# Threshold attention and a two-layer projection: TensorE in 64-row tiles from the fourth quad on, projections in two phases of half rows

## The chip, the cores and the metric

One core of one Trainium2 chip. The metric is the device time of one execution in microseconds (us), median of the runs. A run more than 1.5% above the fastest of its kernel counts as slow and is left out of ratios, though not out of the medians. The experiments ran in three sets, on three chips, so between sets only the ratios compare, each to the kernel before in the same rounds.

## The reference

Attention over 8 batches of 8 heads, 576 positions, head size 64. Scores further than tau = 0.02 below their row's maximum are set to -1e9 ahead of the softmax. The result, 4608 tokens of 512, goes through two projections with a gate between.

```python
scores = scale * q @ k.T
thresh = max(scores, -1) - tau
scores = where(scores >= thresh, scores, -1e9)
attn = exp(scores - max(scores)); attn /= attn.sum(-1) + 1e-9
x = (attn @ v)                      # to tokens x 512
h = x @ w_in                        # 512 -> 2048
g = h * clip(h + 3, 0, 6) / 6
out = g @ w_out                     # 2048 -> 512
```

## The kernel before

Two heads make a pair, two pairs a quad; there are 16 quads. A quad has nine slots, each with the scores of 128 query rows for two heads (the ninth has the last 64 rows of all four heads, and no first-projection item). All engines work through the slots in order, and each slot carries pieces of other work: one item of the first projection (two 128-row blocks of h, 256 or 320 tokens wide), a quarter of an output tile of the second projection, a key transpose or an attention product.

```python
# scores: contraction over 64, two heads at once in two 64-row tiles of the array
nc.tensor.matmul(tiles[a][:, hf, 0:HALF], qT_of(pair)[a*64:(a+1)*64, t*P:(t+1)*P], keys(pair, a, hf), ...)

def mm1(item, pool=None):                       # first projection, full 128 rows
    hps = (pool or ps_h).tile([P, 2, 512], F32, ...)      # the one h buffer, two banks
    for n in range(2):
        for ki in range(KI):
            nc.tensor.matmul(hps[:, n, 0:w], w_in_sb[:, ki, ...], xT[b][:, ki, c0:c0 + w], ...)

# slot n, in the order of the text (each engine keeps its own part of it)
sm_exp(prev); sm_max(sl)                        # ACT; DVE maxima, GpSimd bias
h = mm1(item); r = mm1_relu(h, on_act=...); mm1_gate(item, h, r)   # PE; ACT or DVE; DVE
sm_recip(prev)                                  # DVE
mm2_part(bb, mt, part)                          # PE, a quarter of an output tile
sm_mask(sl)                                     # ACT, waits for the bias
# ... key transpose or attention product, and its eviction
queue[n + 1].tiles = scores(...)                # PE
sm_norm(prev)                                   # GpSimd
```

The program lays out PSUM, the memory that TensorE writes its results to, in this way: four banks for scores, two for h, one for output tiles, one for transposes and attention products.

## Time and profile before

| | before |
|---|---|
| time, median of 3 runs | 562.7 us (562.25 to 563.66) |
| span of the profiled run | 562.3 us |
| busy share PE / ACT / DVE / GpSimd | 95% / 84% / 75% / 54% |
| a quad in the middle of the run | 31.4 us, of which PE 31, ACT 28.4 to 29.1 |

How to read it: the records of TensorE's products overlap (in the prediction's lines, a group that starts at 301.62 and lasts 1.25 us is still on when the next starts at 302.71), so 95% says that TensorE seldom stands still, not that it multiplies at its peak. PE is TensorE, ACT ScalarE, DVE VectorE and POOL GpSimd; `h<-xT,w_in_sb` reads "writes h from xT and w_in_sb". The lines themselves are in the prediction.

### The profile page before, as it was taken

The page shows a single profiled execution, that of the slowest core. Times are in us where ns is not written, and L with a number is a line of the kernel's source. Part 1 is how long each engine was busy: PE and PEld are TensorE (multiplying, and loading weights), DVE is VectorE, ACT ScalarE, POOL GpSimd, SP SyncE. Part 2 cuts the span into 40 slices and gives each one's busy share as a digit, 9 for nine tenths or more (in the row PEclk, how much of TensorE's full clock was granted, in tenths as well). Part 3 has the DMA queues.
Part 4 walks back from the last instruction along what each step waited for, and adds up shares of the span by engine and source line. Part 5 has one row for each costly group of instructions (what it writes and reads, how often), then busy time and mean ns, then how long its engine had stood idle before and what let it go on. Part 6 is the DMA issues. An engine that isn't in the chain of part 4 may idle for free.

```text
span 562.3 us, 11634 instructions
## 1 busy us (share of the span) xinstructions
PE 535.0 (95%) x3856; PEld 309.3 (55%) x3856; DVE 424.4 (75%) x1040; ACT 470.3 (84%) x999; POOL 305.2 (54%) x646
## 2 busy tenths in 40 slices
PE   7998798899999999999999999999999999999997
PEld 5665455455545565555555565655555565654663
DVE  3588787687878788787878798887978798883440
ACT  4799899798988999989898999899898999983540
POOL 1678878854556555655456555755556555561000
PEclk8899999899999999999999999999999999999999
DMA  5879999997689876978589867987699865453102
GB/s 110 135 110 166 162 160 184 207 148 144 112 159 153 151 153 127 208 139 155 114 150 170 159 137 146 174 160 146 127 137 175 167 124 117 101 109 86 38 20 75
DMA packets 286204, 77.52 MB, mean 138 GB/s; under 512 B 269248, under 2 KB 281536, under 8 KB 286144
## 3 DMA queue, kind: packets, MB, share of 16 engines
q1 hardware_dynamic: 268736, 67.86, 64.8%
q0 software_dynamic: 17408, 8.92, 13.7%
q8 instruction: 30, 0.49, 0.4%
q14 instruction: 30, 0.25, 0.2%
HBM read 36.70 MB, written 9.44 MB: 82 GB/s over the span
## 4 chain that ended last, share of the span: by engine, by line
PE 58%; DVE 11%; ACT 9%; issue 4%; POOL 1%; DMA 1%; SPq 1%; DVEq 0%; POOLq 0%
PE h L353 18%; PE o L382 17%; PE s L256 16%; DVE s L277 5%; ACT s L285 4%; PE av L323 3%; ACT s L290 3%; DVE g L370 2%; DVE r L364 2%; ACT r L362 2%; PE s L262 1%; PE tp L213 1%; PE ar L323 1%; DVE osb L390 1%; POOL pn L298 1%
## 5 line engine op out<-in xcount | busy, mean ns | idle before, releaser
L298 POOL TENSOR_SCALAR pn<-s,rinv 128x576 bf16<-128x576 f32 x288 | 211.6, 745 | 133.5 <-issue 58.5
L277 DVE TENSOR_SCALAR_CACHE_REDUCE s<-s 128x576 f32<-128x576 f32 x288 | 205.9, 752 | 44.9 <-PE s L256 35.2
L285 ACT ACTIVATE s<-s,bias 128x576 f32<-128x576 f32 x288 | 207.1, 766 | 36.8 <-POOL bias L280 35.7
L290 ACT ACTIVATE s<-s 128x576 f32<-128x576 f32 x288 | 192.7, 671 | 0.3
L256 PE MATMUL s<-kT,qT 64*128 64x288 f32 x1024 | 172.7, 435 | 5.4 <-DVE s L277 3.2
L353 PE MATMUL h<-xT,w_in_sb 128*128 128x320 bf16 (+1 forms) x1024 | 145.0, 287 | 5.5 <-DVE g L370 4.6
L382 PE MATMUL o<-w_out_sb,g 128*128 128x512 bf16 x576 | 140.9, 379 | 3.6 <-DVE osb L390 3.0
L353 PEld LDWEIGHTS <-w_in_sb 128*128 128x128 bf16 x1024 | 92.0, 97 | 68.4 <-issue 31.1
L256 PEld LDWEIGHTS s<-kT,qT 64*128 64x128 f32 x1024 | 94.8, 188 | 62.7 <-DVE s L277 24.9
L370 DVE SCALAR_TENSOR_TENSOR g<-r,h 128x512 bf16<-128x512 f32 (+1 forms) x128 | 96.4, 754 | 41.2 <-ACT r L362 39.3
L280 POOL TENSOR_SCALAR bias<-m 128x1 f32<-128x1 f32 x288 | 54.4, 189 | 69.0 <-DVE s L277 48.2
L382 PEld LDWEIGHTS <-g 128*128 128x128 bf16 x576 | 55.6, 98 | 58.2 <-issue 9.8
L362 ACT ACTIVATE r<-h,three 128x640 f32<-128x640 f32 (+1 forms) x74 | 54.4, 737 | 21.1 <-PE h L353 20.4
L290 ACT ACTIVATION_READ_ACCUMULATOR s<-s 128x1 f32 x288 | 54.2, 188 | 0.0
L364 DVE TENSOR_SCALAR r<-h 128x512 f32<-128x512 f32 (+1 forms) x54 | 40.5, 751 | 0.0
L390 DVE TENSOR_SCALAR osb<-o 128x512 f32<-128x512 f32 x31 | 21.0, 676 | 22.2 <-PE o L382 22.2
L323 PE MATMUL av<-pT,vm 128*64 128x512 bf16 x256 | 34.6, 392 | 2.0 <-ACT kT L203 2.0
L323 PEld LDWEIGHTS <-vm 128*64 128x64 bf16 x512 | 18.1, 111 | 25.2 <-issue 18.3
L293 DVE RECIPROCAL rinv<-rsum 128x2 f32<-128x2 f32 x144 | 23.0, 160 | 10.2 <-ACT s L290 9.5
L335 DVE CAST xT<-av 128x512 bf16<-128x512 f32 x32 | 21.8, 681 | 5.6 <-PE av L326 5.3
L277 DVE DVE_READ_ACCUMULATOR s<-s 128x1 f32 x288 | 23.9, 83 | 0.0
L388 ACT ACTIVATE osb<-o 128x512 f32<-128x512 f32 x5 | 3.0, 597 | 23.9 <-PE o L382 23.9
(42 smaller groups left out, 255.9 us busy)
## 6 DMA issues: line engine op xcount, KB each, us to landing
km<-in_k_dram SPq DMA_DIRECT2D x64, 128.0 KB, 3.0
out_dram<-osb SPq DMA_DIRECT2D x32, 256.0 KB, 2.4
nq<-in_q_dram SPq DMA_DIRECT2D x96, 72.0 KB, 2.7
vm<-in_v_dram POOLq DMA_DIRECT2D x16, 256.0 KB, 5.4
nq<-in_q_dram SPq DMA_DIRECT2D x16, 128.0 KB, 3.9
w_in_sb<-in_moe_w_in_dram POOLq DMA_DIRECT2D x16, 128.0 KB, 4.1
w_out_sb<-in_moe_w_out_dram POOLq DMA_DIRECT2D x16, 128.0 KB, 4.5
pT<-pn SPq DMA_TRANSPOSE x119, 3.4
```

Of the source, the lines that this page charges most:

```text
L256: nc.tensor.matmul(tiles[a][:, hf, 0:HALF], qT_of(pair)[a * 64:(a + 1) * 64, t * P:(t + 1) * P], keys(pair, a, hf), start=True, stop=True)
L277: nc.vector.tensor_scalar(out=sl.s[:, i, :].rearrange("p (a b) -> p a b", a=2), in0=ps[:, :, 0:HALF], scalar1=1.0, scalar2=None, op0=Alu.m ...
L280: nc.gpsimd.tensor_scalar(out=sl.bias[:, i:i + 1], in0=sl.m[:, i:i + 1], scalar1=-scale, scalar2=tau, op0=Alu.mult, op1=Alu.add)
L285: nc.scalar.activation(out=s, in_=s, func=Act.Prelu, bias=sl.bias[:, i:i + 1], scale=scale, alpha=REJECT)
L290: nc.scalar.activation(out=s, in_=s, func=Act.Exp, accum_out=sl.rsum[:, i:i + 1])
L298: nc.gpsimd.tensor_scalar(out=pn[:, i, :], in0=sl.s[:, i, :], scalar1=sl.rinv[:, i:i + 1], scalar2=1.0, op0=Alu.mult, op1=Alu.mult)
L323: nc.tensor.matmul(ps[a * 64:(a + 1) * 64, :], vm[:, 2 * hp + a, c * D:(c + 1) * D], pT[:, 5 * a + c, cols], start=(c == 0), stop=False)
L353: nc.tensor.matmul(hps[:, n, 0:w], w_in_sb[:, ki, (ni + n) * P:(ni + n + 1) * P], xT[b][:, ki, c0:c0 + w], start=(ki == 0), stop=(ki == KI ...
L362: nc.scalar.activation(out=r, in_=hps, func=Act.Relu, bias=three[:])
L364: nc.vector.tensor_scalar(out=r, in0=hps, scalar1=3.0, scalar2=0.0, op0=Alu.add, op1=Alu.max)
L370: nc.vector.scalar_tensor_tensor(out=gbuf[:, ni:ni + 2, c0:c0 + w], in0=r, scalar=6.0, in1=hps, op0=Alu.min, op1=Alu.mult)
L382: nc.tensor.matmul(o_ps[0], gbuf[:, ni, mt * P:(mt + 1) * P], w_out_sb[:, ni, :], start=(ni == 0), stop=(ni == NI - 1))
```

## The change

The scores use 64-row tiles of the array and all else uses full rows, so TensorE changes its mode twice in every slot. The intent is to keep it in 64-row tiles. Every projection is cut into half rows: row tile 0 and row tile 1 work at the same time into two different banks, then, in a second phase, they swap banks. Between the phases a product must wait for the end of the other tile's products. That wait goes by way of GpSimd: an empty instruction there waits for TensorE, and TensorE waits for it. To fill the wait, other products stand between the two phases.

```diff
+    class Banks:
+        def products(self, phase, insts):
+            follows(insts[0], self)
+            if self.phase not in (None, phase):
+                relay = nc.gpsimd.nop(nofuse=True)
+                tc.add_manual_dep(relay.ins, self.after.ins.name, SYNC, reason="end of a phase")
+                tc.add_manual_dep(insts[0].ins, relay.ins.name, SYNC, reason="next phase")
+            self.phase, self.after = phase, None
+    def mm1_phase(item, hps, phase):
+        for ki in range(KI):
+            for a in range(2):
+                n, c = a ^ phase, row_tile(a)
+                # hps[:, n] += w_in_sb[c, ki, block ni + n].T @ xT[c, ki, tokens]
+        h_banks.products(phase, insts)
+    # mm2_phase: the same for an output tile, in two halves of 256 columns
 # ... slot n, late slots (n >= 27):
+            elif slot == 5:
+                small.append(lambda: av_main(2 * quad - 1))
+                small.append(lambda: av_rest(quad - 1))
+        if late_slot and slot in (0, 3) and todo2:      # first half of an output tile
+        elif late_slot and slot in (1, 4) and mine:     # its second half
+        elif late_slot and slot == 6 and item and len(todo2) > 1:   # a whole one
+        if late_slot and (phases or small):
+            mm1_phase(item, h, 0)
+            mm2_phase(*phases[0][0], phases[0][1], nis)     # or
+            for job in small: evicts.append(job())          # transposes, attention products
+            mm1_phase(item, h, 1)
+            mm2_phase(*phases[-1][0], phases[-1][1], ...)
+        elif item:
+            h = mm1(item)
-            sm_recip(prev)         # behind the gate
+            sm_recip(prev)         # ahead of relu and gate
 # ... relus on ACT in slots 0, 1, 3, 5 become 0, 1, 4, 5; banks "o" and "m" become one tile of two banks
```

More of the change, by code (lines that the diff above doesn't have):

```diff
@@ L43 @@
     N1 = 22
-    N2 = 28
+    N2 = 27
+    DH = d_model // 2
     scale = 1.0 / math.sqrt(D)
@@ L63 @@
     ps_o = ctx.enter_context(tc.psum_pool(name="ps_o", bufs=1))
-    ps_m = ctx.enter_context(tc.psum_pool(name="ps_m", bufs=1))
     ctx.enter_context(tc.manual_schedule())
@@ L189, with bank, row_tile, __init__ @@
     turn = 0
-    def bank(name):
+    obank = ps_o.tile([P, 2, 512], F32, tag="o", name="o")
+    def bank():
         nonlocal turn
         turn += 1
-        if now < N2 and turn % 2:
-            return ps_o.tile([P, 512], F32, tag="o", name=name)
-        return ps_m.tile([P, 512], F32, tag="m", name=name)
+        return obank[:, turn % 2, :]
+    def row_tile(a):
+        return slice(64 * a, 64 * a + 64)
+    SYNC = mybir.DependencyInfo(mybir.DependencyClass.Sync, mybir.DependencyReason.DATA)
+    groups = []
+    class Banks:
+        def __init__(self):
+            self.phase = self.after = None
+            groups.append(self)
+        def products(self, phase, insts):
[5 more added lines that the diff above has]
+            self.phase, self.after = phase, None
+    def follows(inst, banks=None):
+        for one in groups:
+            if one is not banks and one.after is None:
+                one.after = inst
+    h_banks, o_banks = Banks(), Banks()
     def copy_out(out, in_):
@@ L209, in main_pe @@
     def main_pe(src, pair):
-        ps = bank("tp")
+        ps = bank()
         n = pair % 2
@@ L219, in transpose_q @@
             ps = main_pe(nq[:, 0:1024].rearrange("p (t h d) -> p t h d", h=4, t=4), pair)
-            return lambda: nc.vector.tensor_copy(out=qT_of(pair)[:, 0:512], in_=ps[:])
+            return lambda: nc.vector.tensor_copy(out=qT_of(pair)[:, 0:512], in_=ps)
         n = pair % 2
@@ L224, in transpose_k @@
     def transpose_k(pair):
-        ps = main_pe(nat[pair // 2][1], pair)
-        return lambda: copy_out(kT_of(pair)[:, 64:576], ps[:])
+        if now < N2:
+            ps = main_pe(nat[pair // 2][1], pair)
+            return lambda: copy_out(kT_of(pair)[:, 64:576], ps)
+        km, n = nat[pair // 2][1], pair % 2
+        insts = []
+        for t in range(4):
+            for a in range(2):
+                c = row_tile(a)
+                insts.append(nc.tensor.transpose(obank[:, a, t * 64:(t + 1) * 64],
+                                                 km[c, t, 2 * n:2 * n + 2, :], identf[c, c]))
+        o_banks.products(0, insts)
+        return lambda: copy_out(kT_of(pair)[:, 64:576].rearrange("p (t a j) -> p a t j", a=2, j=64),
+                                obank[:, :, 0:256].rearrange("p a (t j) -> p a t j", j=64))
     def transpose_rest(quad):
-        ps = bank("tr")
         nq, _, kr = nat[quad]
-        nc.tensor.transpose(ps[:, 0:P], kr[:], identf[:])
-        if by_pe(2 * quad):
-            nc.tensor.transpose(ps[:, P:2 * P], nq[:, 1024:1152], identf[:])
+        qT, kT = qkT[quad]
+        if now < N2:
+            ps = bank()
+            nc.tensor.transpose(ps[:, 0:P], kr[:], identf[:])
+            if by_pe(2 * quad):
+                nc.tensor.transpose(ps[:, P:2 * P], nq[:, 1024:1152], identf[:])
+            both = ps.rearrange("p (w n t) -> p w n t", n=2, t=64)
+            rest = both[:, 0]
+        else:
+            o_banks.products(0, [nc.tensor.transpose(obank[:, a, 256:320], kr[row_tile(a), :],
+                                                     identf[row_tile(a), row_tile(a)]) for a in range(2)])
+            rest = obank[:, :, 256:320]
         def evict():
-            qT, kT = qkT[quad]
-            both = ps[:].rearrange("p (w n t) -> p w n t", n=2, t=64)
             if by_pe(2 * quad):
                 nc.vector.tensor_copy(out=qT[:, :, 512:S], in_=both[:, 1])
-            copy_out(kT[0:64, :, S:S + 64], both[0:64, 0])
-            copy_out(kT[64:P, :, 0:64], both[64:P, 0])
+            copy_out(kT[0:64, :, S:S + 64], rest[0:64])
+            copy_out(kT[64:P, :, 0:64], rest[64:P])
         return evict
@@ L255, in scores @@
                 for a in range(2):
-                    nc.tensor.matmul(tiles[a][:, hf, 0:HALF], qT_of(pair)[a * 64:(a + 1) * 64, t * P:(t + 1) * P],
-                                     keys(pair, a, hf), start=True, stop=True)
+                    inst = nc.tensor.matmul(tiles[a][:, hf, 0:HALF], qT_of(pair)[a * 64:(a + 1) * 64, t * P:(t + 1) * P],
+                                            keys(pair, a, hf), start=True, stop=True)
+                    follows(inst)
             else:
@@ L261, in scores @@
                         pair = 2 * quad + n
-                        nc.tensor.matmul(tiles[a][n * 64:(n + 1) * 64, hf, 0:HALF],
-                                         qT_of(pair)[a * 64:(a + 1) * 64, 512:S], keys(pair, a, hf),
-                                         start=True, stop=True)
+                        inst = nc.tensor.matmul(tiles[a][n * 64:(n + 1) * 64, hf, 0:HALF],
+                                                qT_of(pair)[a * 64:(a + 1) * 64, 512:S], keys(pair, a, hf),
+                                                start=True, stop=True)
+                        follows(inst)
         return tiles
@@ L322, in av @@
             for a in range(2):
-                nc.tensor.matmul(ps[a * 64:(a + 1) * 64, :], vm[:, 2 * hp + a, c * D:(c + 1) * D],
-                                 pT[:, 5 * a + c, cols], start=(c == 0), stop=False)
+                inst = nc.tensor.matmul(ps[a * 64:(a + 1) * 64, :], vm[:, 2 * hp + a, c * D:(c + 1) * D],
+                                        pT[:, 5 * a + c, cols], start=(c == 0), stop=False)
+                follows(inst)
         for a in range(2):
@@ L331, in av_main @@
             xT[b] = x_pool.tile([P, KI, S], BF16, tag="xT", name="xT")
-        ps = bank("av")
-        av(ps[:], pair, pts[pair], slice(0, 512))
+        ps = bank()
+        av(ps, pair, pts[pair], slice(0, 512))
         o0 = 64 if b % 2 else 0
-        nc.vector.tensor_copy(out=xT[b][:, hp, o0:o0 + 512], in_=ps[:])
+        return lambda: nc.vector.tensor_copy(out=xT[b][:, hp, o0:o0 + 512], in_=ps)
     def av_rest(quad):
         b, g = divmod(quad, 2)
-        ps = bank("ar")
+        ps = bank()
         for n in range(2):
@@ L342, in av_rest @@
         o0 = 0 if b % 2 else 512
-        nc.vector.tensor_copy(out=xT[b][:, 2 * g:2 * g + 2, o0:o0 + 64],
-                              in_=ps[:, 0:P].rearrange("p (a b) -> p a b", a=2))
+        return lambda: nc.vector.tensor_copy(out=xT[b][:, 2 * g:2 * g + 2, o0:o0 + 64],
+                                             in_=ps[:, 0:P].rearrange("p (a b) -> p a b", a=2))
     def mm1(item, pool=None):
@@ L355, in mm1 @@
         return hps[:, :, 0:w]
+    def mm1_phase(item, hps, phase):
+        b, ni, c0, w = item
+        insts = []
+        for ki in range(KI):
+            for a in range(2):
+                n, c = a ^ phase, row_tile(a)
+                insts.append(nc.tensor.matmul(
+                    hps[:, n, 0:w], w_in_sb[c, ki, (ni + n) * P:(ni + n + 1) * P], xT[b][c, ki, c0:c0 + w],
+                    start=(phase == 0 and ki == 0), stop=(phase == 1 and ki == KI - 1)))
+        h_banks.products(phase, insts)
     def mm1_relu(hps, on_act):
@@ L371, in mm1_gate, with mm2_phase, mm2_full, mm2_out @@
                                        op0=Alu.min, op1=Alu.mult)
-    o_ps = {}
-    def mm2_part(bb, mt, part, pool=None):
-        if part == 0:
-            if pool:
-                o_ps[0] = pool.tile([P, 2, 512], F32, tag="s", name="o")[:, 0, :]
-            else:
-                o_ps[0] = ps_o.tile([P, d_model], F32, tag="o", name="o")[:]
-        for ni in range(part * 4, part * 4 + 4):
-            nc.tensor.matmul(o_ps[0], gbuf[:, ni, mt * P:(mt + 1) * P], w_out_sb[:, ni, :],
+    def mm2_phase(bb, mt, phase, nis):
+        insts = []
+        for ni in nis:
+            for a in range(2):
+                j, c = a ^ phase, row_tile(a)
+                insts.append(nc.tensor.matmul(
+                    obank[:, j, 0:DH], gbuf[c, ni, mt * P:(mt + 1) * P], w_out_sb[c, ni, j * DH:(j + 1) * DH],
+                    start=(phase == 0 and ni == 0), stop=(phase == 1 and ni == NI - 1)))
+        o_banks.products(phase, insts)
+    def mm2_full(bb, mt, ps):
+        for ni in range(NI):
+            nc.tensor.matmul(ps, gbuf[:, ni, mt * P:(mt + 1) * P], w_out_sb[:, ni, :],
                              start=(ni == 0), stop=(ni == NI - 1))
-    def mm2_out(bb, mt, on_act):
+    def mm2_out(bb, mt, on_act, ps=None):
         osb = o_pool.tile([P, d_model], F32, tag="osb", name="osb")
+        dst = osb[:]
+        if ps is None:
+            ps, dst = obank[:, :, 0:DH], dst.rearrange("p (j c) -> p j c", j=2)
+            o_banks.phase = None
         if on_act:
-            nc.scalar.activation(out=osb[:], in_=o_ps[0], func=Act.Copy, scale=1.0 / 6.0)
+            nc.scalar.activation(out=dst, in_=ps, func=Act.Copy, scale=1.0 / 6.0)
         else:
-            nc.vector.tensor_scalar_mul(out=osb[:], in0=o_ps[0], scalar1=1.0 / 6.0)
+            nc.vector.tensor_scalar_mul(out=dst, in0=ps, scalar1=1.0 / 6.0)
         b0 = 2 * bb * S
@@ L412, in moe_of @@
                 items.append(((b, ni, c0, w), ()))
-            items[-1] = (items[-1][0], [(b // 2, mt, part) for mt in mts for part in range(4)])
+            items[-1] = (items[-1][0], [(b // 2, mt) for mt in mts])
         return items
@@ L431 @@
     queue[0].tiles = scores(0, 0)
-    prev = None
+    prev = mine = None
     for n, sl in enumerate(queue):
@@ L447 @@
             load_v(b + 1)
+        copies = pe_transpose(queue[n - 2]) if n > 1 and queue[n - 2].on_chip else None
+        late_slot = n >= N2
+        nxt = 2 * quad + 2
+        more = quad + 1 < NQUAD
+        vector, small = [], []
+        if slot == (6 if late_slot else 5) and more:
+            alloc_qk(quad + 1)
+            vector.append(lambda: transpose_q(nxt))
+        if late_slot:
+            if slot == 0:
+                vector.append(lambda: transpose_q(2 * quad + 1))
+            elif slot == 2:
+                small.append(lambda: transpose_k(2 * quad + 1))
+            elif slot == 5:
+                small.append(lambda: av_main(2 * quad - 1))
+                small.append(lambda: av_rest(quad - 1))
+            elif slot == 7 and more:
+                small.append(lambda: transpose_k(nxt))
+                small.append(lambda: transpose_rest(quad + 1))
+        else:
+            if slot == (1 if quad else 2):
+                vector.append(lambda: transpose_q(2 * quad + 1))
+            elif slot == (2 if quad else 3):
+                small.append(lambda: transpose_k(2 * quad + 1))
+            elif slot == 3 and quad > 0:
+                small.append(lambda: av_main(2 * quad - 1))
+            elif slot == 4 and quad > 0:
+                small.append(lambda: av_rest(quad - 1))
+            elif slot == 6:
+                small.append(lambda: transpose_k(nxt))
+            elif slot == 7:
+                small.append(lambda: transpose_rest(quad + 1))
@@ new lines @@
+        if slot == 8:
+            small.append(lambda: av_main(2 * quad))
+        item = None
+        if slot != 8 and todo1:
+            item, then = todo1.pop(0)
+        phases = []
+        if late_slot and slot in (0, 3) and todo2:
+            mine = todo2.pop(0)
+            phases = [(mine, 0)]
+        elif late_slot and slot in (1, 4) and mine:
+            phases, mine = [(mine, 1)], None
+        elif late_slot and slot == 6 and item and len(todo2) > 1:
+            one = todo2.pop(0)
+            phases = [(one, 0), (one, 1)]
@@ new lines @@
+        evicts = []
+        if late_slot and (phases or small):
+            if item:
+                h = ps_h.tile([P, 2, 512], F32, tag="h", name="h")
+                mm1_phase(item, h, 0)
+            if phases:
+                nis = range(16 if len(phases) == 2 else 4)
+                mm2_phase(*phases[0][0], phases[0][1], nis)
+            for job in small:
+                evicts.append(job())
+            if item:
+                mm1_phase(item, h, 1)
+                h = h[:, :, 0:item[3]]
+            if phases:
+                mm2_phase(*phases[-1][0], phases[-1][1], range(nis.stop % NI, NI))
+        elif item:
+            h = mm1(item)
@@ L451 @@
         sm_max(sl)
-        if slot != 8 and todo1:
-            item, then = todo1.pop(0)
-            h = mm1(item)
-            r = mm1_relu(h, on_act=(slot in (0, 1, 3, 5)))
-            mm1_gate(item, h, r)
-            todo2.extend(then)
-        copies = pe_transpose(queue[n - 2]) if n > 1 and queue[n - 2].on_chip else None
         if prev is not None:
@@ L463 @@
             copies()
+        if item:
+            r = mm1_relu(h, on_act=(slot in ((0, 1, 4, 5) if late_slot else (0, 1, 3, 5))))
+            mm1_gate(item, h, r)
+            todo2.extend(then)
         outs = []
-        pieces = 0 if slot == 3 else 1
-        if slot == 0:
-            second = True
-        if second and slot < 2 and len(todo2) > 1 and todo2[0][1] == todo2[1][1]:
-            pieces, second = 2, False
-        for _ in range(pieces):
-            if todo2:
-                bb, mt, part = todo2.pop(0)
-                mm2_part(bb, mt, part)
-                if part == 3:
-                    outs += mm2_out(bb, mt, on_act=False)
+        for one, phase in phases:
+            if phase == 1:
+                outs += mm2_out(*one, on_act=False)
         for i in range(2):
             sm_mask(sl, i)
-        evict = None
-        nxt = 2 * quad + 2
-        if slot == (1 if quad else 2):
-            evict = transpose_q(2 * quad + 1)
-        elif slot == (2 if quad else 3):
-            evict = transpose_k(2 * quad + 1)
-        elif slot == 3 and quad > 0:
-            av_main(2 * quad - 1)
-        elif slot == 4 and quad > 0:
-            av_rest(quad - 1)
-            if quad % 2 == 0:
-                todo1.extend(moe_of(quad // 2 - 1))
-        elif slot in (5, 6, 7) and quad + 1 < NQUAD:
-            if slot == 5:
-                alloc_qk(quad + 1)
-                evict = transpose_q(nxt)
-            elif slot == 6:
-                evict = transpose_k(nxt)
-            else:
-                evict = transpose_rest(quad + 1)
-        elif slot == 8:
-            av_main(2 * quad)
-        if evict:
+        for job in vector:
+            evict = job()
+            if evict:
+                evict()
+        if not late_slot:
+            evicts = [job() for job in small]
+        for evict in evicts:
             evict()
+        if slot == (5 if late_slot else 4) and quad > 0 and quad % 2 == 0:
+            todo1.extend(moe_of(quad // 2 - 1))
         if n + 1 < len(queue):
@@ L535, in rest2 @@
         while todo2:
-            bb, mt, part = todo2.pop(0)
-            mm2_part(bb, mt, part, pool=ps_s if count[1] % 3 else None)
-            if part == 3:
-                flush()
-                late.extend(mm2_out(bb, mt, on_act=(count[1] % 2 == 0)))
-                count[1] += 1
+            one = todo2.pop(0)
+            c = count[1] % 4
+            ps = ps_s.tile([P, 2, 512], F32, tag="s", name="o")[:, 0, :] if c % 2 else obank[:, c // 2, :]
+            mm2_full(*one, ps)
+            flush()
+            late.extend(mm2_out(*one, on_act=(count[1] % 2 == 0), ps=ps))
+            count[1] += 1
     for item in todo1:
         rest1(*item)
-    av_main(2 * last + 1)
+    av_main(2 * last + 1)()
     rest2()
-    av_rest(last)
+    av_rest(last)()
     for item in moe_of(B - 1):
```

## The prediction

> **What bounds the kernel now.** I read the page first (busy shares, the 40 slices, the chain that ended last), then the stretches of five quads in the middle of the run, then the chain and the timeline of a few slots. A quad is 4 heads of one batch; it has 9 slots, each a tile of softmax scores for two heads, with a first-projection item and a piece of the second projection hung into it.
>
> ```profile
> PE 535.0 (95%) x3856; PEld 309.3 (55%) x3856; DVE 424.4 (75%) x1040; ACT 470.3 (84%) x999; POOL 305.2 (54%) x646
> ```
>
> TensorE is busy nearly all the time, but ScalarE is not far behind. The stretches run from one quad's last score tile to the next one's:
>
> ```profile
> 282.44:313.76 31.32, 31.20 (x230) 17.70 (x229) 26.17 (x65) 28.41 (x63) 19.10 (x39) 1.00 0.99 157
> 376.18:408.10 31.92, 31.89 (x230) 17.55 (x229) 26.76 (x64) 29.14 (x63) 16.68 (x37) 1.00 0.70 142
> ```
>
> The columns after the length are busy us of PE, weight loads, DVE, ACT and POOL. A quad takes about 31.4 us (mean of the last twelve), PE is busy for all of it, ACT for 28.4 to 29.1. ACT's records overlap a little; by start-to-start times a slot costs ACT 2.66 (two exps 1.33, two masks 1.33), and with four relus (0.63) and the key copies (1.45 a quad) 28.0 a quad. That is the floor however fast TensorE gets: 3.4 us a quad could be gained at most.
>
> The chain of waits agrees that TensorE's own order sets the pace:
>
> ```profile
> 317.71 1.17 PE s L256 x8
> 318.88 0.98 PE h L353 x8
> 319.86 1.73 PE o L382 x8
> 321.59 1.17 PE s L256 x8
> 322.76 0.98 PE h L353 x8
> 323.74 0.86 PE o L382 x4
> ```
>
> Scores (s), first projection (h), second projection (o), nothing between. Beside it runs a loop through the only h buffer: projection, relu, gate, next projection. Its terms:
>
> ```profile
> 299.94 0.77 ACT L362 ACTIVATE r<-h,three 128x640 f32<-128x640 f32 x1
> 300.75 0.82 DVE L370 SCALAR_TENSOR_TENSOR g<-r,h 128x640 bf16<-128x640 f32 x1 [1.11 <-ACT r L362]
> 301.62 1.25 PE L353 MATMUL h<-xT,w_in_sb 128*128 128x320 bf16 x8
> 302.71 0.38 PE L382 MATMUL o<-w_out_sb,g 128*128 128x512 bf16 x1
> ```
>
> Relu start to gate start 0.81, gate start to the next projection 0.87, a 320-wide projection 1.09 in TensorE time, its last result some 0.17 after that: 2.9 us (3.0 where DVE does the relu). TensorE's own slot is longer, 1.17+1.09+0.86 = 3.1 and more, so the loop is hidden today.
>
> **What the Trainium skill says.** "TensorEngine Tiling (Array Packing)", Key Properties: changing the tiling mode drains TensorE. The trace agrees: score pairs (64-row tiles) start 0.242 us apart, but from the last pair to the first full-row projection it is 0.335, so 0.09 goes to the drain. On the way in, the last 512-column product holds 0.216 and the first pair starts 0.309 later (0.09 again), and the second pair comes 0.347 after the first, as its weights could not be loaded ahead (0.105 more). A round trip costs 0.29 us. The same page, Gotcha 1: different row tiles cannot write one PSUM bank at the same time. Hence the two phases with a wait between; no run yet shows it. "TensorE: Matmul & The Clock Gate", What overlaps and what doesn't: matmuls end in order, which lets the wait be hung on the first matmul after a phase. "Advanced Engine Details and Errata", Sequencer Loop: control instructions run in the sequencer while engine instructions sit in the queue; so GpSimd's relay should not have to wait for its 0.745 us normalisations to end. The trace before has no relay.
>
> **The change part by part.** The first three quads hardly change (they have no second projection), nor does the tail: one first-projection item more is left for it (+1.1), a quarter of a 3.45 us output tile less (-0.9). So the case is decided by 13 quads.
>
> Removed: mode switches. In the built program 80 of the 106 projection items of the loop run in half rows. Seven slots a quad lose up to 0.29 us, those with attention products (128x64 mode, slots 5 and 8) keep theirs, and slots 3 and 4 fall back to full rows in 10 of 13 quads, as no output tile is waiting. That leaves 4 to 5 slots, 1.3 us a quad. Key transposes in half rows: 0.44 becomes some 0.22 twice, 0.4 a quad. On TensorE alone -1.7 us a quad, -22 us in all.
>
> Unchanged on TensorE: the products. A pair of half-row matmuls should hold the array as long as one full-row matmul (score pairs start 7 ns apart): an output tile is 32 pairs x 0.109 = 3.49 against 16 x 0.216 = 3.45.
>
> Added: 187 relays. Each asks for the first result of the following group (0.27 after its start) plus two semaphore hops, which I put at 0.2. Behind it lie 0.44 us of other products in slots 0 and 1, 0.22 in slot 2. So 0.1 to 0.3 us of stall five times a quad: about +1.
>
> Moved: this is what decides. The products between the two phases now stretch the h loop, and the output tiles are bunched: slots 0 and 1 take one, slot 6 a whole one in every quad. I take for each slot the longer of TensorE's own work and the h loop, 320-wide items, two output tiles a quad:
> slots 0 and 1: 1.09 + half a tile 1.74 + scores 0.97 + relay 0.1 = 3.9 each (loop 3.46);
> slot 2: loop 1.09+0.22+0.3+0.17+0.85+0.86 = 3.4;
> slots 3 and 4: loop 3.0 each;
> slot 5: both attention products lie between the phases (1.10+0.36, switches 0.2), so the loop is 1.09+1.66+0.17+0.80+0.86 = 4.6, and ACT, which does this relu, waits for it;
> slot 6: 1.09+3.49+0.97 = 5.55, plus 0.3 as its output banks must first be emptied by DVE (0.59+0.20 after the gate, against half an item 0.54), 5.9;
> slots 7 and 8: 1.09+0.28+0.3+0.97 and 1.10+0.28+0.97 = 5.0, plus about 0.7 because slot 8's attention product goes to the banks that ACT empties only after slot 7's masks.
> Sum 7.8+3.4+6.0+4.6+5.9+5.7 = 33.4. Quads with 256-wide items are shorter (8 x 0.22 on projections), those with a third tile longer in slots 3 and 4 (2 x 0.8). Weighing them, about 32.7 against 31.4 now. The same rule gives 31.5 for today's kernel. So 13 x 1.3 = +17 us: 580.
>
> **The rivals.** First, TensorE's own work is the pace: then 13 x (-1.7 + 1.0 of relay stalls), -9 us, or with relays fully hidden -22: 541 to 554. For it speak the 95% busy share and the chain; against it that ACT is within 3 us of the bound and that with one h buffer TensorE can't run ahead of gates. Slot 6 has 5.9 us of TensorE work against 2.7 of ACT's, slots 7 and 8 4.7 against 6.3, and neither can store that up. Second, GpSimd's relays become the wait: they stand ahead of the bias in its order, and ACT's masks wait for the bias already.
>
> ```profile
> ACT s L285 <- POOL bias L280: 35.7, 72, 1.9
> ```
>
> If a relay takes 0.5 instead of 0.2, five a quad, that is 13 x 1.5 = +20 more, near 600. Against that: the reciprocal moves ahead of the gate on DVE, so normalisations start earlier and leave the way to the bias free, which could give some of the 35.7 back. Third, half-row weight loads (97 ns each, two per 109 ns) might not overlap; an output tile would then take nearly twice its time, +3.5 a quad per tile and more: over 650. The score loads start 6 ns apart in the trace, so I give this 3%.
>
> **Range and chances.** The slot sums say 580. A careful rearrangement of this size was hardly made without a reason to expect a gain, and the sums take waits one at a time, so I shade to 577. One us per quad is 13 us: the low end, 547, is the first rival at -1.2 a quad, the high end, 599, is the sum with slower relays. The 2% marks are 551.4 and 574.0. Faster 0.2, same 0.25, slower 0.55.
>
> **What would show it.** Right: quads near 32.7 us; slot 6 near 6 us and slots 3 and 4 near 3; new TensorE idle time before h (waiting for gates), before the attention product of slot 8 (waiting for key copies) and before second halves (waiting for GpSimd); ACT's share down, with relus waiting for h in slot 5; score pairs still 0.242 apart but no 0.29 lost in slots 0, 1, 2 and 7; half-row pairs 0.109 apart. Wrong: quads under 30.6 with TensorE busy throughout (first rival), relays stalling TensorE 0.5 us or more (second), pairs spaced 0.2 apart (third).

## The result, and the profile after

The changed kernel takes 591.4 us (median of 4 runs, 585.2 to 597.3) against 562.7: it is slower. The ratio is 1.047, with a 95% interval of 1.039 to 1.055. Ratios here are the mean time of one kernel's fast runs over that of the other's of the same rounds, so not quite the ratio of the medians. One of the four runs (597.3) is slow and not in it. The profiled run is a fast one. First the busy shares of its page:

```profile
PE 533.5 (90%) x5949; PEld 377.0 (64%) x5952; DVE 427.6 (73%) x1041; ACT 468.8 (79%) x998; POOL 305.2 (52%) x646
```

TensorE's busy sum is practically what it was, in 27 us more time. Two quads from the middle, in the same columns as before (length, then busy us of PE, weight loads, DVE, ACT, POOL):

```profile
395.23:429.28 34.05, 30.86 (x383) 22.22 (x378) 26.95 (x65) 28.94 (x63) 16.63 (x37) 1.00 0.71 130
429.28:462.96 33.68, 30.65 (x384) 22.04 (x378) 26.69 (x65) 28.95 (x63) 19.35 (x41) 1.00 0.86 149
```

A quad takes 34 us, ACT is busy for the same 29, and PE is no longer busy for all of it. By the start times of the score products the 27.5 us between the two profiles divide so: up to the fourth quad +1.5, the fourth quad itself +4.2 (35.5 to 39.7), the eleven quads after it +19.2, the last one +1.8, the tail +0.7. The first of these cannot be put down to the change: among the profiles of kernels that share the changed kernel's way up to there it took from 91.0 to 94.0 us, and before 92.5.

The mean length of a slot over those eleven quads, from the last score product of one slot to that of the next:

| slot | 0 | 1 | 2 | 3 | 4 | 5 | 6 | 7 | 8 | sum |
|---|---|---|---|---|---|---|---|---|---|---|
| before | 3.84 | 3.29 | 3.56 | 3.58 | 3.64 | 3.15 | 3.66 | 3.27 | 3.58 | 31.55 |
| after | 3.71 | 3.71 | 2.86 | 3.23 | 3.19 | 3.81 | 6.54 | 3.03 | 3.23 | 33.30 |

Slots 5 and 6 lose 0.66 and 2.88 us and slot 1 loses 0.42, more than the others win. A slot does not hold the same work before and after: slot 1 now has half an output tile and mostly had a quarter, slot 6 has a whole one, slot 5 has both attention products, which were in slots 3 and 4. So the table shows where the quad grew, and not yet why. The time in which TensorE stood idle ahead of its products is plainer: 0.5 us a quad before and 2.4 after. Of these, 0.3 each in slots 3 and 4, 0.2 in slot 5 and 0.75 in slot 6 are nearly all waits for a gate, and 0.8 in slot 8 is the attention product waiting for ACT's key copies.

First a slot that went as intended, slot 0 of a quad, on TensorE's timeline (start, length, instruction):

```profile
332.74 0.60 PE L417 MATMUL h<-xT,w_in_sb 64*128 64x256 bf16 x8
333.18 0.60 PE L443 MATMUL o<-w_out_sb,g 64*128 64x256 bf16 x8
333.61 0.60 PE L417 MATMUL h<-xT,w_in_sb 64*128 64x256 bf16 x8
334.05 1.48 PE L443 MATMUL o<-w_out_sb,g 64*128 64x256 bf16 x24
335.36 1.14 PE L307 MATMUL s<-kT,qT 64*128 64x288 f32 x8
336.33 0.60 PE L417 MATMUL h<-xT,w_in_sb 64*128 64x256 bf16 x8
```

Four pairs of half-row products take 0.44 us, 0.109 a pair, so the two row tiles do work side by side. The second phase (333.61) comes when the 0.43 us of other work is done, so the relay is hidden. From scores to projection it is 0.97 where it was 1.17: the mode switch is gone. Now slots 5 and 6 of the same quad, again TensorE alone:

```profile
350.37 0.62 PE L417 MATMUL h<-xT,w_in_sb 64*128 64x256 bf16 x8
350.92 1.05 PE L376 MATMUL o<-pT,vm 128*64 128x512 bf16 x8
351.81 0.38 PE L380 MATMUL o<-pT,vr 128*64 128x512 bf16 x2
...
352.43 0.61 PE L417 MATMUL h<-xT,w_in_sb 64*128 64x256 bf16 x8
352.88 1.14 PE L307 MATMUL s<-kT,qT 64*128 64x288 f32 x8
354.55 0.89 PE L417 MATMUL h<-xT,w_in_sb 64*128 64x256 bf16 x8 [0.53 <-DVE g L435]
355.35 1.92 PE L443 MATMUL o<-w_out_sb,g 64*128 64x256 bf16 x32
357.09 0.62 PE L417 MATMUL h<-xT,w_in_sb 64*128 64x256 bf16 x8
357.53 1.93 PE L443 MATMUL o<-w_out_sb,g 64*128 64x256 bf16 x32
359.27 1.15 PE L307 MATMUL s<-kT,qT 64*128 64x288 f32 x8
```

Slot 5's item begins at 350.37 and its second phase only at 352.43, as both attention products lie between. What hangs on it is on ACT's and DVE's timelines:

```profile
353.09 0.69 ACT L427 ACTIVATE r<-h,three 128x512 f32<-128x512 f32 x1 [1.44 <-PE h L417]
353.81 0.69 DVE L435 SCALAR_TENSOR_TENSOR g<-r,h 128x512 bf16<-128x512 f32 x1 [1.63 <-ACT r L427]
354.41 0.68 DVE L389 CAST xT<-o 128x512 bf16<-128x512 f32 x1
355.01 0.28 DVE L397 CAST xT<-o 128x128 bf16<-128x128 f32 x1
355.21 0.75 DVE L330 TENSOR_SCALAR_CACHE_REDUCE s<-s 128x576 f32<-128x576 f32 x1
```

ACT stands idle 1.44 us for h, DVE 1.63 for the relu. Then TensorE waits 0.53 us for the gate, which frees h. The evictions of the attention products (the two CASTs) are behind the gate in DVE's order, and the maxima of slot 6, whose scores had ended at 354.02, before the gate did, are behind those. The chain of waits shows the same place in the quad before, one link after another (start, length, link):

```profile
318.38 0.67 PE h L417 x8
...
319.07 0.80 ACT r L427
...
320.64 0.68 DVE xT L389
321.32 0.21 DVE xT L397
321.53 0.04 issue
321.57 1.92 PE o L443 x32
```

Before, such a stretch of the chain was TensorE alone. Here ACT and DVE stand in it.

### The profile page after: what moved, and what is told of

It reads as the page before. It is cut to its first block, busy times and chain, and to the rows that moved or that the text cites. A ratio compares the mean times of both kernels' runs of the same rounds, so it can differ in the third digit from the quotient of the medians.

```text
span 589.8 us, 15943 instructions
## 1 busy us (share of the span) xinstructions
PE 533.5 (90%) x5949; PEld 377.0 (64%) x5952; DVE 427.6 (73%) x1041; ACT 468.8 (79%) x998; POOL 305.2 (52%) x646
## 4 chain that ended last, share of the span: by engine, by line
PE 50%; DVE 14%; ACT 13%; issue 5%; DMA 2%; POOL 1%; SPq 0%; DVEq 0%; POOLq 0%
PE o L443 16%; PE h L417 9%; PE s L307 9%; DVE s L330 6%; ACT s L338 6%; PE h L407 5%; PE o L376 5%; PE o L450 5%; DVE g L435 3%; ACT r L427 3%; ACT s L343 3%; DVE r L429 2%; ACT kT L237 2%; DMA pR<-pn 2%; DVE xT L389 1%
## 5 line engine op out<-in xcount | busy, mean ns | idle before, releaser
L307 PEld LDWEIGHTS s<-kT,qT 64*128 64x128 f32 x1024 | 104.8, 189 | 41.1 <-DVE s L330 17.6
L417 PE MATMUL h<-xT,w_in_sb 64*128 64x256 bf16 (+1 forms) x1280 | 107.2, 284 | 15.7 <-DVE g L435 10.6
L443 PE MATMUL o<-w_out_sb,g 64*128 64x256 bf16 x1792 | 112.6, 269 | 0.9 <-DVE xT L397 0.6
L443 PEld LDWEIGHTS <-g 64*128 64x128 bf16 x1792 | 94.3, 94 | 7.9 <-issue 2.3
L417 PEld LDWEIGHTS <-w_in_sb 64*128 64x128 bf16 x1280 | 61.9, 94 | 45.5 <-issue 21.7
L407 PE MATMUL h<-xT,w_in_sb 128*128 128x320 bf16 (+1 forms) x384 | 53.0, 288 | 12.1 <-DVE g L435 12.0
L407 PEld LDWEIGHTS <-w_in_sb 128*128 128x128 bf16 x384 | 35.4, 98 | 33.1 <-DVE g L435 17.2
L376 PE MATMUL o<-pT,vm 128*64 128x512 bf16 x256 | 34.6, 391 | 11.2 <-ACT kT L237 10.8
L376 PEld LDWEIGHTS <-vm 128*64 128x64 bf16 x512 | 21.2, 111 | 31.9 <-issue 23.4
L450 PE MATMUL o<-w_out_sb,g 128*128 128x512 bf16 x125 | 27.8, 379 | 1.3 <-DVE xT L389 1.1
```

The source lines that it names most:

```text
L307: inst = nc.tensor.matmul(tiles[a][:, hf, 0:HALF], qT_of(pair)[a * 64:(a + 1) * 64, t * P:(t + 1) * P], keys(pair, a, hf), start=True, sto ...
L376: inst = nc.tensor.matmul(ps[a * 64:(a + 1) * 64, :], vm[:, 2 * hp + a, c * D:(c + 1) * D], pT[:, 5 * a + c, cols], start=(c == 0), stop=F ...
L407: nc.tensor.matmul(hps[:, n, 0:w], w_in_sb[:, ki, (ni + n) * P:(ni + n + 1) * P], xT[b][:, ki, c0:c0 + w], start=(ki == 0), stop=(ki == KI ...
L417: insts.append(nc.tensor.matmul(hps[:, n, 0:w], w_in_sb[c, ki, (ni + n) * P:(ni + n + 1) * P], xT[b][c, ki, c0:c0 + w], start=(phase == 0 ...
L443: insts.append(nc.tensor.matmul(obank[:, j, 0:DH], gbuf[c, ni, mt * P:(mt + 1) * P], w_out_sb[c, ni, j * DH:(j + 1) * DH], start=(phase == ...
L450: nc.tensor.matmul(ps, gbuf[:, ni, mt * P:(mt + 1) * P], w_out_sb[:, ni, :], start=(ni == 0), stop=(ni == NI - 1))
```

## The experiments

Twelve kernels ran. "A quad" below is the mean of the eleven quads after the fourth, from the trace of each run; the changed kernel has 33.30 and the kernel before 31.55.

**Spread the output tiles.** In 10 of 13 quads slot 6 takes a whole output tile while slots 3 and 4 have none.

```diff
-        elif late_slot and slot == 6 and item and len(todo2) > 1:
+        elif late_slot and slot == 6 and item and len(todo2) > 2:
```

> One number changed: slot 6 takes a whole output tile only when more than two are waiting, so that slots 3 and 4 take the second tile of most quads. My theory (the bunched order and the single h buffer make the loss): in the 10 quads that change, slots 3 and 4 go from 3.0 to about 3.75 us each, slot 6 from 6.6 to about 3.2, so some 2 us a quad, 20 us in all: near 571 us. Rival (half rows or relays themselves are dear): moving a tile to other slots gives nothing, 585 or more.

Measured: 588.3 us (median of five, of which two are slow; the fast ones are 582.9, 583.8 and 588.3), ratio 1.036 (1.031 to 1.041); a quad 33.02. A miss: some 20 us were expected and a few came. In a quad that changed, slot 6 fell from 7.03 to 4.16 and not to 3.2, and slot 3 rose from 3.0 to 4.5 and not to 3.75. The bunched tile is not the main loss. Something holds slot 6 without it.

**No relays.** Wrong result on purpose: each row tile keeps its bank in both phases, so no wait is needed.

```diff
-                n, c = a ^ phase, row_tile(a)
+                n, c = a, row_tile(a)
# the same in mm2_phase; the relay and its two dependencies are taken out
```

> Wrong result on purpose: each row tile keeps its own bank in both phases, so no relay is needed and all 187 are gone; the number and shape of the products stay. My theory: relays stall TensorE by 0.1 us in slots 2 and 7 and not at all elsewhere, and hold the bias of slot 6 a little: 586 to 591 us. Rival (the relays, or GpSimd's order behind them, make the loss): 570 or less.

Measured: 587.1 us, ratio 1.043 (1.039 to 1.048), not distinguishable from the changed kernel; a quad 33.28. As my theory had it, for the quads in question. The profiles differ in one place, the fourth quad: 35.7 us without relays, 39.7 with them. There the changed kernel's TensorE and, next, its GpSimd show (the bracket is the idle time ahead of the line and what ended it):

```profile
115.85 1.25 PE L417 MATMUL h<-xT,w_in_sb 64*128 64x320 bf16 x8 [4.07 <-POOLq L220]
```

```profile
115.77 1.47 POOL L351 TENSOR_SCALAR pn<-s,rinv 128x576 bf16<-128x576 f32 x2 [4.65 <-DMA pR<-pn]
```

GpSimd's normalisation waits for a transposing DMA to free its buffer, and the relay of TensorE's next phase stands behind that wait: TensorE idles 4.07 us. In the whole run this is the only wait of a product for a relay that the profile shows. It does not price the relays: SyncE gave out the transposing DMA from 105.01 to 110.55 here, and from 102.94 to 106.46 without relays, as the query loads before it held SyncE longer here (4.26 against 2.53 us). The profile of the spread tiles has such a stall too (3.72 us), but that of the early evictions below, with all its relays, has none, and a fourth quad of 35.4 us. Why the loads were slow in this execution is not shown, and what the same late DMA would have cost without relays was not measured.

**The changed order, in full rows.** Every projection and key transpose as before, at the places of the changed kernel.

```diff
-                n, c = a ^ phase, row_tile(a)          # half rows, both banks
+        n = phase                                      # full rows, one bank a phase
# output tiles: 16 products of 512 columns, 8 in each phase, in one bank
```

> The order of the changed kernel, but every projection and key transpose in full rows, with no relay (the first half of an item is its first bank, the second half its second). My theory: the order alone makes the loss, and the mode switches come back on top: slot 6 stays above 6.5 us, 590 to 608 us in all. Rival (half rows make the loss): back near 563 to 575.

Measured: 595.6 us, ratio 1.057 (1.053 to 1.061); a quad 34.02, slot 6 6.50. As my theory had it: without any half row or relay the changed order is slow (all its moves together; the places of the reciprocal and of the relus were not tested alone). Half rows are worth 0.72 us a quad in it, and 0.28 each in slots 0 and 1, where TensorE sets the pace.

**Slot 5's item ahead of the attention products, tiles spread.**

```diff
+        if late_slot and slot == 5:
+            if item:
+                h = mm1(item)
+            for job in small:
+                evicts.append(job())
-        if late_slot and (phases or small):
+        elif late_slot and (phases or small):
```

> As e1_spread, and in slot 5 the projection item whole and in full rows, with the attention products behind it instead of between its halves. My theory: ScalarE gets slot 5's h some 1.5 us earlier, slot 5 and the start of slot 6 shrink by 0.5 to 1 us together, 13 times: 6 to 12 us below e1_spread, near 562. Rival (slot 5 is bound by something else, such as TensorE's sum): within 3 us of e1_spread.

Measured: 571.7 us, ratio 1.015 (1.012 to 1.018); a quad 32.11. The gain over the spread tiles is as expected, 0.91 us a quad, or 12 us by the two ratios. The 562 us are missed by 10, as they stood on the 571 us that the spread tiles did not reach. Slot 6 is down to 2.86 where it has no tile.

**The same, tiles left where they were.**

> The changed kernel with slot 5's projection item whole and in full rows ahead of its attention products, and the output tiles left where they were (slot 6 takes one in every quad). It completes the square with e1 (tiles spread) and e4 (both). My theory after the first runs: the item stretched by the attention products in slot 5 is the larger loss, about 0.7 to 1.2 us a quad by itself: 575 to 583 us. Rival (the two only work together, the bunched tile covers slot 5's loss): within 3 us of 588.

Measured: 575.7 us, ratio 1.023 (1.021 to 1.026); a quad 32.33. So of the square, spreading the tiles alone is worth 0.28 us a quad, slot 5 alone 0.97, both 1.19: the stretched item of slot 5 is the larger cause by far. On TensorE's timeline the end of slot 5 and the begin of slot 6, still with its whole tile:

```profile
343.03 1.24 PE L307 MATMUL s<-kT,qT 64*128 64x288 f32 x8
344.10 0.60 PE L417 MATMUL h<-xT,w_in_sb 64*128 64x256 bf16 x8
344.54 1.91 PE L443 MATMUL o<-w_out_sb,g 64*128 64x256 bf16 x32
```

The projection follows the scores in 1.07 us, where the changed kernel needs 1.67.

**Free h earlier.** Wrong result on purpose: the gate multiplies r by r, so h is free once the relu has read it.

```diff
-    ... scalar=6.0, in1=hps, op0=Alu.min, op1=Alu.mult)
+    ... scalar=6.0, in1=r,   op0=Alu.min, op1=Alu.mult)
```

> Wrong result on purpose: the gate multiplies r by itself instead of by h, so h is free once the relu has read it, some 0.8 us sooner; counts and orders of all instructions stay. My theory (the loop through the one h buffer sets the pace in slots 3 to 6): the waits of projections for the gate go, 1.5 to 2.5 us a quad, 560 to 572 us. Rival (TensorE's own work and ScalarE's wait for masks set it): 585 or more.

Measured: 584.0 us, ratio 1.039 (1.037 to 1.041); a quad 33.14. A miss. The wait for the gate is gone, but slot 6 is as long as it was (6.55 us in the mean, against 6.54). Its timeline on TensorE shows why:

```profile
348.04 0.49 PE L417 MATMUL h<-xT,w_in_sb 64*128 64x256 bf16 x6
349.34 0.29 PE L417 MATMUL h<-xT,w_in_sb 64*128 64x256 bf16 x2 [0.81 <-DVE xT L389]
```

In this quad and every other one slot 6 starts on a new batch, and its first item reads what the evictions write. In the quads between, the output tile waits for the same evictions instead, about 1 us each time, as they empty its banks. Slots 3 and 4 got no shorter either (3.26 and 3.31 against 3.23 and 3.19), though their waits for the gate, 0.3 us each, are gone too. My account of the loop through h alone falls: in slot 6 there is a second wait beside it.

**Evictions ahead of the gate.** The changed kernel with slot 5's two evictions moved ahead of the relu and gate, where DVE is idle anyway.

```diff
+        if late_slot and slot == 5:
+            for evict in evicts:
+                evict()
+            evicts = []
         if item:
             r = mm1_relu(h, ...)
```

> The changed kernel with one thing moved: in slot 5 VectorE empties the attention products' banks ahead of the gate instead of behind it (it stands idle 1.4 us there, waiting for the relu). Since freeing h early (e6) gave nothing in slot 6, I now take it that two waits lie side by side there: the gate, and behind it in VectorE's order the evictions that slot 6's inputs, banks and maxima need. New theory: with the evictions ahead, the second wait goes, slot 6 from 6.4-7.0 to about 6.0, 0.4 to 0.6 us a quad, 580 to 585 us. Rival (slot 6 is TensorE's own work alone, the waits are hidden): within 3 us of 588.

Measured: 583.2 us, ratio 1.037 (1.031 to 1.044); a quad 32.96, slot 6 6.20: 0.34 us a quad, a little less than expected. On the timeline of slot 6 the first wait is there and the second is not (the item takes 0.61 us, and took 0.89):

```profile
345.75 0.61 PE L417 MATMUL h<-xT,w_in_sb 64*128 64x256 bf16 x8 [0.53 <-DVE g L435]
346.18 1.93 PE L443 MATMUL o<-w_out_sb,g 64*128 64x256 bf16 x32
```

**Both.** Wrong result on purpose, as above.

> Wrong result on purpose: e9_evict and e6_hfree together, so both waits of slot 6 are gone. New theory: slot 6 comes down to TensorE's own 5.5 us, 0.9 to 1.3 us a quad below the changed kernel, 572 to 578 us, clearly more than the sum of e9's and e6's own gains. Rival (no pair of waits; each acts alone): the sum of their gains, or nothing.

Measured: 569.8 us, ratio 1.014 (1.010 to 1.017); a quad 32.07. The early h alone gave 0.16 us a quad and the early evictions 0.34; together they give 1.23. Slot 6 is at 5.3 to 5.7, with no wait in front of its item:

```profile
341.21 1.14 PE L307 MATMUL s<-kT,qT 64*128 64x288 f32 x8
342.18 0.60 PE L417 MATMUL h<-xT,w_in_sb 64*128 64x256 bf16 x8
342.62 1.91 PE L443 MATMUL o<-w_out_sb,g 64*128 64x256 bf16 x32
```

That is far more than the sum of the two, as the pair of waits has it: each hides the other, and only without both does slot 6 shrink to TensorE's own work.

**Both, and no relays.** In slot 6 the changed kernel's bias comes late behind a relay, and ACT's masks wait for it:

```profile
357.56 0.47 POOL L333 TENSOR_SCALAR bias<-m 128x1 f32<-128x1 f32 x2 [3.61 <-PE h L417]
```

```profile
357.78 1.44 ACT L338 ACTIVATE s<-s,bias 128x576 f32<-128x576 f32 x2 [1.35 <-POOL bias L333]
```

> Wrong result on purpose: e10_both with the relays gone as in e2_norelay. In slot 6 the bias stands behind the second relay in GpSimd's order and came 1.6 us after its maximum. Theory: ScalarE's masks of slot 6 come earlier, but the next scores are TensorE's to give, so at most 3 us below e10. Rival (the bias behind the relay is the next wait in line): 8 us or more below e10.

Measured: 572.7 us, ratio 1.019 (1.013 to 1.024); a quad 32.15. The intervals of this run and the one before overlap: no gain to be seen. So ACT's 1.35 us wait is real but costs nothing that this run can show. That ACT would only wait later instead, for the next scores, is my reading and was not measured.

**Key copies ahead of the masks.** On top of the spread tiles and slot 5's item: in slots 2 and 7 ACT copies the transposed keys first.

```diff
+        if late_slot and slot in (2, 7):
+            for evict in evicts:
+                evict()
+            evicts = []
         for i in range(2):
             sm_mask(sl, i)
```

> As e4_slot5, and ScalarE's copies of the keys in slots 2 and 7 stand ahead of that slot's masks. My theory: the attention product of slot 8 stops waiting for the copies (0.8 us) and the tile of slot 3 for its banks; 0.6 to 1.2 us a quad, 557 to 565 us. Rival (ScalarE only shifts its own work, the masks come later and so do the next scores' exps): within 3 us of e4_slot5's 571.7.

Measured: 569.4 us, ratio 1.013 (1.011 to 1.015); a quad 31.73. Less than expected: slot 8 fell from 3.23 to 2.95, and slot 3 not at all. By the times alone the rival stands: 569.4 is within 3 us of 571.7, and the two intervals overlap. The gain, 0.38 us a quad, is seen in the traces only, where TensorE's wait of 0.8 us for the key copies is gone. The quads are now within 0.2 us of the kernel before. What remains is mostly the tail, 63.8 us from the last score product to the end against 60.3: the new rule for slot 6 leaves one output tile more, which I had not counted in this expectation nor in that of the spread tiles.

**Another relu on ACT.** Slot 2's relu to ACT, slot 5's to DVE.

> As e7_copies, with the relu of slot 2 on ScalarE and that of slot 5 on VectorE. My theory: in slot 2 VectorE's maxima, relu and gate in a row (3.1 us) outlast TensorE's 2.2 us and hold slot 3 by 0.7; that goes, and slot 5 has enough other work: 4 to 8 us below e7. Rival (ScalarE, with relu and key copy in slot 2, becomes the wait there): equal to e7 or slower.

Measured: 573.4 us, ratio 1.016 (1.011 to 1.022); a quad 31.95. No gain, as the rival had it: slot 3 gains 0.2 us and slot 4 loses 0.4, as about half of TensorE's wait for a gate ahead of slot 3's item went, and as much came ahead of slot 4's. Whether ScalarE is the cause, as the rival said, is not shown.

**One tile less for the tail.** As the key copies, but the last quad's slot 6 takes any tile that waits.

> As e7_copies (correct), but in the last quad slot 6 takes a tile if any waits, so that one 3.45 us tile less is left for the tail; in the loop it costs some 2 to 2.5. Expected 1 us below e7, 566 to 570, still not below the kernel before.

Measured: 565.0 us (563.8 to 567.5), ratio 1.005 (1.001 to 1.009), correct. This is the best of the half-row kernels, and it does not beat the kernel before. The edit itself gained nothing in the traces: the tail is 2.7 us shorter than with the key copies and the last quad 2.5 longer. What else lies between the two profiled runs (565.4 and 562.0 us, on two chips) comes in and before the fourth quad.

## Why the prediction was right

The call (slower, 577 us, 547 to 599) holds: 591.4. By its own steps:

- **Which bound.** That TensorE set the pace held: in the kernel before it idles 0.5 us in a quad of 31.55. ACT's floor of 28.0 was not tested, as no run came near it. The rival in which TensorE's busy sum decides (541 to 554) is out: the busy sum stayed at 533.5 us while the time rose.
- **Removed: mode switches.** The 0.29 us a slot is right where TensorE sets the pace: 0.28 in slots 0 and 1. The sum of 1.7 a quad, transposes included, was too much; 0.72 arrived. That other waits took its place elsewhere fits, but no run tested it.
- **Unchanged: the products.** Pairs start 0.109 us apart, as the step had it. The third rival (loads of half rows that do not overlap) is out.
- **Added: relays.** Over-sized for the quads: 0.1 to 0.3 us, five times a quad, was the estimate; without relays a quad is 0.02 shorter. The reading that a relay does not wait for normalisations to end held: at 357.83 one went ahead of two of them that had not begun, the first at 358.12. But it was too simple: a relay does stand behind the wait that a normalisation can bring with it, as in the fourth quad, where a late DMA made that wait long and TensorE idled 4.07 us. The profile of the early evictions shows that this need not happen.
- **Moved: the order.** This step named the right slots. (Its slot 2 is summed wrongly: the terms make 3.49 and not 3.4.) Against a quad with two output tiles and 320-wide items in slots 0 to 7:

| slots | 0, 1 | 2 | 3, 4 | 5 | 6 | 7 + 8 | sum |
|---|---|---|---|---|---|---|---|
| predicted | 7.8 | 3.4 | 6.0 | 4.6 | 5.9 | 5.7 | 33.4 |
| measured | 7.6 | 2.9 | 6.0 | 4.3 | 7.0 | 6.3 | 34.1 |

  The term that was mis-sized is slot 6: I gave 0.3 us to emptying its banks. The measured extra over TensorE's own 5.55 is 1.5, from the late gate and from the evictions behind it: in every other quad, as here, these write inputs of slot 6, which I had not seen, and in the quads between they empty the banks. The prediction also named the loop through the h buffer as the mechanism; the early-h run shows that it is only one of two waits side by side, the evictions behind the gate being the other. Both hang on the same thing, the late end of slot 5's item. In slots 3 and 4 the loop's 3.0 us fit, but freeing h early did not shorten them, so there the number is no proof of the mechanism. The wait of slot 8 for the key copies was right, 0.8 us against about 0.7.
- **The sum.** +1.75 us a quad against +1.3, hence 19.2 us over eleven quads, plus the 4.2 us of the fourth quad, which the prediction did not have. Part of the agreement is luck: slots 0, 1, 2 and 5 were put 1.0 us too long together and slots 6 to 8 1.7 too short. The step down from 580 to 577 went the wrong way.

What stays open: in the best half-row kernel slot 3 still lasts 4.0 to 4.5 us where TensorE's work is 3.6 to 3.8. Neither the earlier key copies nor the other relu removed it. The trace with the key copies shows TensorE idle for 0.4 us ahead of slot 3's item, for the gate of slot 2; no run took that wait away.

## What to carry to other kernels

Filling a wait on one engine with other products lengthens the life of whatever they interrupt: here a projection of 0.9 us took 2.7 us from first to last product, and two other engines stood still for it, for 1.4 and 1.6 us. Put the fillers where nobody waits for the thing they split, or finish it first and pay the mode switch. When taking one wait away changes nothing, look for a second one beside it and take both away before dropping the theory.

## What the Trainium skill lacked or had wrong

- "TensorEngine Tiling (Array Packing)", Key Properties, says that a mode switch drains TensorE but gives no size. Here it is 0.09 us each way and 0.105 for the weights that are not loaded ahead, 0.29 a round trip; removing it saved 0.28 in slots 0 and 1.
- The same page, Gotcha 1, leaves the synchronisation of row tiles to software and names no means. The relay by way of GpSimd is free when 0.43 us of other products cover it, in slot 0 above. A wait of GpSimd's own ahead of it held TensorE for 4.07 us, once.
- "Advanced Engine Details and Errata", Sequencer Loop, does not say what a control instruction waits for. Here the relay passed normalisations that had not begun (357.83 against 358.12), but stood behind a wait that the program carries as an instruction of its own, ahead of a normalisation (an EVENT_SEMAPHORE that ended at 115.65; the relay ran at 115.78). Other pages of the skill do tell of such inserted waits, so this is a gap of the page and not of the skill.
